# Attention plus gated FFN on one core: FFN matmuls moved from 128-row to 64-row tiles, score work cut into single units, first batch reordered

## The chip, the cores and the metric

The kernel runs on one core of one Trainium2 chip. The metric is device time in microseconds (us) of one execution, smaller is better. The names of the engines in the profile are: PE = TensorE (matmul), PEld = TensorE's weight load, DVE = VectorE, ACT = ScalarE, POOL = GpSimd, SP = SyncE, which issues most DMAs here.

## The reference

Eight batches of eight heads, sequence 576, head size 64. Causal attention with a decay per position, then a gated FFN (512 to 1536 to 512) over all 4608 tokens, in fp32 at the interface:

```python
def _attn_ref(q, k, v, f):                      # q, k, v: [8, 8, 576, 64], f: [8, 8, 576]
    scores = scale * np.matmul(q, k.transpose(0, 1, 3, 2))
    cum = np.cumsum(np.log(np.clip(f, 0.0001, 1.0)), axis=-1)
    scores = np.where(causal, -1e9, scores + cum[:, :, :, None] - cum[:, :, None, :])
    scores = scores - np.max(scores, axis=-1, keepdims=True)
    attn = np.exp(scores)
    attn = attn / (np.sum(attn, axis=-1, keepdims=True) + 1e-09)
    return np.matmul(attn, v)

def _moe_ref(x, w_gate, w_val, w_out):          # x: [4608, 512]
    return (1.0 / (1.0 + np.exp(-(x @ w_gate))) * (x @ w_val)) @ w_out
```

## The kernel before

The tokens are cut into nine FFN chunks of 512. While the FFN of chunk c runs, the attention of batch c+1 is slipped in between its matmul groups ("steps", 36 a chunk: 24 first-layer steps, 12 second-layer steps). Batches 0 and 1 are partly ahead; chunks 7 and 8 are pure FFN. Heads go in pairs, four pairs a batch.

The scores of a pair are cut into four pieces, the units A to D. They contract over the head size of 64, so the two heads stand in the two 64-row halves of the array. The FFN contracts over 128 rows.

```python
def Q_mm(p, u, sc):                       # scores: 64 rows, two heads side by side
    qT, kT = st[p, "q"], st[p, "k"]
    for jt, i0, i1, c in UNITS[u]:
        for h in range(2):
            hp = slice(64 * h, 64 * h + 64)
            nc.tensor.matmul(ps[:, sc + h, c:c + i1 - i0],
                             kT[hp, jt * NP:(jt + 1) * NP], qT[hp, i0:i1], start=True, stop=True)
...
def burst1(p):                            # two units (C and A) in one burst
    Q_mm(p, "C", 3)
    Q_mm(p, "A", 0)
    Q_exp(p, "C", 3)
    later.append(lambda: (Q_exp(p, "A", 0), vg_step(p)))
...
def burst3(p):                            # attention product of two pairs, then normalisation
    ...
    nc.vector.transpose(Z, psf[:, o:o + S])          # row sums to partitions
    nc.vector.reciprocal(r[:, 0, :], ...)
    ...                                              # copies between quadrants
    spread(1)
    later.append(one)                                # scale pair p+1
    later.append(two)                                # scale pair p
...
def g1(ft, w, kind):                      # FFN, first layer: 128 rows, one bank of three in turn
    bk = next_bank()
    for mt in range(NMT):
        nc.tensor.matmul(ps[:, bk, :], w[:, mt, ft * NP:(ft + 1) * NP],
                         xT[:, mt, t0:t0 + TCH], start=(mt == 0), stop=(mt == NMT - 1))
    if kind == "g":
        nc.scalar.activation(sg, ps[:, bk, :], ACTF.Tanh, scale=0.5)
    else:                                 # the gate product
        nc.vector.scalar_tensor_tensor(out=gv[:, ft, :], in0=hold["sg"], scalar=1.0,
                                       in1=ps[:, bk, :], op0=ALU.add, op1=ALU.mult)
...
put((0, 2, 4, 6, 9) if c == 1 else (-1, 0, 3, 6, 9), P)      # steps of the five bursts of a pair of pairs
put((15, 18, 21, 24, 27), P + 2)
```

The cuts are marked with "...".

The softmax here doesn't subtract the row's maximum and nothing guards it: scores larger than these inputs give would overflow.

Of the kernel before, what the change touches and what calls it, by code (L numbers as in the profile page):

```python
# [8 lines left out]
FP32 = mybir.dt.float32  # L9
# [6 lines left out]
def kernel(  # L16
# [14 lines left out]
    NP = 128  # L31
# [3 lines left out]
    NPAIR = BH // 2  # L35
    HPAIR = H // 2
    scale = 1.0 / float(D) ** 0.5
    TPP = 6
    QP = S // TPP

# [3 lines left out]
    NMT = DM // NP  # L44
    NFT = DF // NP
    TCH = 512
    NTC = T // TCH
    C0 = 256
# [10 lines left out]
    gsb = ctx.enter_context(tc.tile_pool(name="gv", bufs=2))  # L59
    pp = ctx.enter_context(tc.tile_pool(name="ps", bufs=1, space=bass.MemoryType.PSUM))  # L60

    ps = pp.tile([128, 8, 512], FP32, tag="ps", name="ps")

    ident_bf = singles.tile([128, 128], BF16, tag="ident_bf", name="ident_bf")
    ident_f = singles.tile([64, 64], FP32, tag="ident_f", name="ident_f")
    g_bf = singles.tile([128, NJT, BH], BF16, tag="g_bf", name="g_bf")
    xT = singles.tile([128, NMT, T], BF16, tag="xT", name="xT")
    wg_bf = singles.tile([128, NMT, DF], BF16, tag="wg_bf", name="wg_bf")
    wv_bf = singles.tile([128, NMT, DF], BF16, tag="wv_bf", name="wv_bf")
    wo_bf = singles.tile([128, NFT, DM], BF16, tag="wo_bf", name="wo_bf")  # L70
    NKT = 4
    kts = [singles.tile([128, SPAD], BF16, tag=f"kt{i}", name=f"kt{i}") for i in range(NKT)]
    NXB = 3
    qns = [singles.tile([128, 2, NJT, 2 * D], BF16, tag=f"qn{i}", name=f"qn{i}") for i in range(NXB)]
    kns = [singles.tile([128, 2, NJT, 2 * D], BF16, tag=f"kn{i}", name=f"kn{i}") for i in range(NXB)]
    NVB = 3
    vbs = [singles.tile([128, NJT, 4, D], FP32, tag=f"vb{i}", name=f"vb{i}") for i in range(NVB)]

    f_nat = singles.tile([BH, S], FP32, tag="f_nat", name="f_nat")
    cum = singles.tile([BH, S], FP32, tag="cum", name="cum")  # L80
# [5 lines left out]
    qtiles, ktiles = {}, {}  # L86

    def load_qk(b, hf, npiece):
        key = (b, hf)
        qt = qk_pool.tile([QP, 4, TPP * D], BF16, tag="qt", name="qt")  # L90
        kt = qk_pool.tile([QP, 4, TPP * D], BF16, tag="kt_in", name="kt_in")
        w = 4 // npiece
        for s in range(npiece):
            for src, dst in ((q, qt), (k, kt)):
                hs = slice(4 * hf + w * s, 4 * hf + w * s + w)
                nc.gpsimd.dma_start(
                    dst[:, w * s:w * s + w, :],
                    src[b, hs].rearrange("h (p t) d -> p h (t d)", t=TPP))
        qtiles[key], ktiles[key] = qt, kt
# [50 lines left out]
    def load_w1(gi):  # L150
        cs = slice(gi * 512, gi * 512 + 512)
        for src, dst in ((moe_w_gate, wg_bf), (moe_w_val, wv_bf)):
            nc.gpsimd.dma_start(dst[:, :, cs],
                                src.rearrange("(m p) c -> p m c", p=NP)[:, :, cs])

    def load_w2(gi):
        nc.gpsimd.dma_start(
            wo_bf[:, 4 * gi:4 * gi + 4, :],
            moe_w_out.rearrange("(m p) c -> p m c", p=NP)[:, 4 * gi:4 * gi + 4, :])


    st = {}
    later = []

    def flush():
        if later:
            later.pop(0)()
# [5 lines left out]
    def T_step(p, which, bk, copy):  # L173
        b, hf, ho = half_of(p)
        src = (qtiles if which == "q" else ktiles)[(b, hf)]
        bank = ps[:, bk, 0:S // 2].bitcast(BF16)
        for t in range(TPP):
            for h in range(2):
                nc.tensor.transpose(  # L179
                    bank[64 * h:64 * h + 64, t * QP:(t + 1) * QP],  # L180
                    src[:, ho + h, t * D:(t + 1) * D], ident_bf[0:QP, 0:QP])
        if which == "q":
            dst = tsb.tile([128, S], BF16, tag="qT", name="qT")
        else:
            dst = kts[p % NKT]
        st[p, which] = dst
        copy(dst[:, 0:S].rearrange("p (n t) -> p n t", t=TPP),
             bank.rearrange("p (t n) -> p n t", t=TPP))

# [7 lines left out]
    UW = {"A": 448, "B": 384, "C": 448, "D": 320}  # L197

    def Q_mm(p, u, sc):
        qT, kT = st[p, "q"], st[p, "k"]  # L200
        for jt, i0, i1, c in UNITS[u]:
            for h in range(2):
                hp = slice(64 * h, 64 * h + 64)
                nc.tensor.matmul(ps[:, sc + h, c:c + i1 - i0],  # L204
                                 kT[hp, jt * NP:(jt + 1) * NP], qT[hp, i0:i1],
                                 start=True, stop=True)

    def Q_exp(p, u, sc):
# [25 lines left out]


# [17 lines left out]
    def AV_mm(p, b0, b1, b2):  # L253
        av(p, CH0, b0, C0, False)
        av(p, CH0, b0, 0, True)
        av(p, CH1, b2, 0, True)
        av(p, CH1, b1, 0, False)

    def norm_r(p, b0, b1, b2):
        NB = S // 32  # L260
        Z = nsb.tile([128, S], FP32, tag="Z", name="Z")
        nc.vector.transpose(Z[:, 0:C0], ps[:, b0, 0:C0])
        nc.vector.transpose(Z[:, C0:S], ps[:, b2, 0:C1])
        r = nsb.tile([128, NB], FP32, tag="r", name="r")
        nc.vector.reciprocal(r, Z.rearrange("p (n c) -> p n c", c=32)[:, :, 0])
        R = nsb.tile([128, S], FP32, tag="R", name="R")
        nc.vector.transpose(R.rearrange("p (n c) -> p n c", c=32),
                            r.unsqueeze(2).to_broadcast([128, NB, 32]))
        st[p, "R"] = R

    def norm_m(p, b0, b1, b2):
        b, a = divmod(p, HPAIR)
        psf = ps.rearrange("p b c -> p (b c)")
        o = b0 * 512 + C0
        nc.vector.tensor_tensor(out=xT[:, a, b * S:(b + 1) * S], in0=psf[:, o:o + S],
                                in1=st[p, "R"], op=ALU.mult)


    def early_pair(p):
        Q_mm(p, "A", 0)  # L280
        Q_exp(p, "A", 0)
        Q_mm(p, "C", 2)
        Q_exp(p, "C", 2)
        if p + 1 < HPAIR:
            T_step(p + 1, "q", 4, nc.scalar.copy if p % 2 else nc.vector.tensor_copy)
            T_step(p + 1, "k", 7, nc.vector.tensor_copy)
        vg_step(p)
        if p:
            early_av(p - 1)
        Q_mm(p, "B", 0)  # L290
        Q_exp(p, "B", 0)
        Q_mm(p, "D", 2)
        Q_exp(p, "D", 2)

    def early_av(p):
        AV_mm(p, 5, 6, 7)
        norm_r(p, 5, 6, 7)
        norm_m(p, 5, 6, 7)


    def burst0(p, b0, b1):
        T_step(p, "k", b0, nc.scalar.copy)
        T_step(p, "q", b1, nc.scalar.copy)

    def burst1(p):
        Q_mm(p, "C", 3)
        Q_mm(p, "A", 0)
        Q_exp(p, "C", 3)
        later.append(lambda: (Q_exp(p, "A", 0), vg_step(p)))

    def burst2(p):
        Q_mm(p, "B", 3)
        Q_mm(p, "D", 0)
        Q_exp(p, "B", 3)
        later.append(lambda: Q_exp(p, "D", 0))
# [3 lines left out]
    def burst3(p):  # L319
        NB = S // 32  # L320
        psf = ps.rearrange("p b c -> p (b c)")
        for ch, bank, off in ((CH0, 3, C0), (CH1, 4, 0)):
            n = len(ch)
            for x, (u, c, w, jt, oc) in enumerate(ch):
                for qd in range(4):
                    pr, h = p + qd % 2, qd // 2
                    nc.tensor.matmul(  # L327
                        ps[32 * qd:32 * qd + 32, bank, off + oc:off + oc + w],
                        g_bf[:, jt, 2 * pr + h:2 * pr + h + 1].to_broadcast([128, 32]),
                        st[pr, u][:, h, c:c + w], start=(x == 0), stop=(x == n - 1),  # L330
                        skip_group_check=True, tile_position=(0, 32 * qd))
        for pr, ch, bank, off in ((p + 1, CH0, 0, C0), (p + 1, CH1, 1, 0),
                                  (p, CH0, 0, 0), (p, CH1, 2, 0)):
            n = len(ch)
            for x, (u, c, w, jt, oc) in enumerate(ch):
                for qd in range(4):
                    h = qd // 2
                    nc.tensor.matmul(  # L338
                        ps[32 * qd:32 * qd + 32, bank, off + oc:off + oc + w],
                        st[pr, "vg"][:, jt, h, 32 * (qd % 2):32 * (qd % 2) + 32],  # L340
                        st[pr, u][:, h, c:c + w], start=(x == 0), stop=(x == n - 1),
                        skip_group_check=True, tile_position=(0, 32 * qd))
        Z = nsb.tile([128, S], FP32, tag="Z", name="Z")
        o = 3 * 512 + C0
        nc.vector.transpose(Z, psf[:, o:o + S])  # L345
# [198 lines left out]
```

## Time and profile before

| reading | value | view |
|---|---|---|
| median time, 4 runs | 396.68 us (396.58 to 399.07) | times |
| TensorE busy | 94% of 396.0 us | page, part 1 |
| FFN matmul, 512 columns, start to start (its pitch) | 0.216 us | timeline, pure FFN chunks |
| pure FFN chunk | 31.1 us | timeline |
| chunk with attention | 40.9 us | timeline |
| chunk 1 begins | 82.6 us | timeline |

Of the page of the kernel before, these are TensorE's busy time beside that of the other engines (us, share of the span of 396.0 us, instructions), and one row of its second part, where each digit is one fortieth of the span: the granted clock of TensorE in tenths of full speed (9 is 90% or more).

```profile
PE 370.3 (94%) x3165; PEld 174.8 (44%) x3165; DVE 163.7 (41%) x320; ACT 191.8 (48%) x286; POOL 210.8 (53%) x341
...
PEclk9988999999999999999999999999999999999999
```

TensorE is the bound, and its clock never falls after the start.

This is TensorE's timeline of the kernel before, in a chunk with attention. The columns are the start, the time until the end, engine and line, operation, tiles, shapes, count, and in brackets the idle time before and what ended it. L392 is the FFN's first layer, L204 the scores.

```profile
183.26 1.02 PE L392 MATMUL ps<-xT,wg_bf 128*128 128x512 bf16 x4 [0.71 <-DVE gv L399]
184.22 0.56 PE L204 MATMUL ps<-xq,xk 64*128 64x448 bf16 x6
184.70 1.04 PE L392 MATMUL ps<-xT,wv_bf 128*128 128x512 bf16 x4
185.58 1.03 PE L392 MATMUL ps<-xT,wg_bf 128*128 128x512 bf16 x4
186.44 1.03 PE L392 MATMUL ps<-xT,wv_bf 128*128 128x512 bf16 x4
187.40 0.47 PE L204 MATMUL ps<-xq,xk 64*128 64x320 bf16 x6
187.81 1.04 PE L392 MATMUL ps<-xT,wg_bf 128*128 128x512 bf16 x4
```

Read the starts, since ends overlap. Four FFN matmuls without a burst behind them take 0.86 (185.58 to 186.44). From 183.26 to 184.70 is 1.44, and from 186.44 to 187.81 is 1.37. So a score burst costs 0.58 and 0.51. Its columns at the FFN's pitch are 896 and 704 (the two heads run side by side), 0.37 and 0.29 us. About 0.22 us is lost at each burst, eight times a chunk. The Trainium skill, "TensorEngine Tiling (Array Packing)", Key Properties, says that changing the tiling mode drains TensorE; the trace agrees and gives the size.

TensorE's waits in the kernel before: what was waited for, us in total, times, longest us. This line is the longest one of the steady chunks.

```profile
PE ps L392 <- DVE gv L399: 4.3, 6, 0.8
```

### The profile page before, as it was taken

How to read it: one execution, taken by the hardware profiler on the slowest of the kernel's cores; microseconds unless marked ns; L12 is line 12 of the kernel's file. 1: busy time of each engine (PE TensorE's matmuls, PEld its weight loads, DVE VectorE, ACT ScalarE, POOL GpSimd, SP SyncE). 2: the span in 40 equal slices, each digit the busy share in tenths (PEclk: the TensorE clock that was granted, in tenths of full speed). 3: DMA queues.
4: the chain of work that ended last, by engine and by line, in shares of the span. 5: the costliest groups of instructions: out<-in, count | busy, mean ns of one | idle time of the engine just before them, and what ended most of it. 6: DMA issues, size and time to landing. Idle time of an engine off the chain costs nothing.

```text
span 396.0 us, 8068 instructions
## 1 busy us (share of the span) xinstructions
PE 370.3 (94%) x3165; PEld 174.8 (44%) x3165; DVE 163.7 (41%) x320; ACT 191.8 (48%) x286; POOL 210.8 (53%) x341
## 2 busy tenths in 40 slices
PE   3867999899999999999999999999999999999995
PEld 2543444434354534443444445444544454444442
DVE  5464245245543453346252725273527252421320
ACT  5651757464545555464637363727273723323321
POOL 8774184959494949494949494848580410000000
PEclk9988999999999999999999999999999999999999
DMA  9999995899776996798679987996860011002002
GB/s 159 196 200 204 196 161 32 124 177 134 97 81 117 183 86 82 100 196 100 62 112 184 121 65 111 153 154 60 90 130 7 0 55 55 0 26 81 1 23 86
DMA packets 141319, 41.59 MB, mean 105 GB/s; under 512 B 128928, under 2 KB 136608, under 8 KB 141280
## 3 DMA queue, kind: packets, MB, share of 16 engines
q0 software_dynamic: 65616, 14.17, 40.7%
q1 hardware_dynamic: 75664, 26.90, 32.0%
q8 instruction: 25, 0.41, 0.4%
q14 instruction: 14, 0.11, 0.1%
HBM read 37.90 MB, written 9.44 MB: 120 GB/s over the span
## 4 chain that ended last, share of the span: by engine, by line
PE 79%; DVE 9%; POOL 5%; ACT 4%; issue 3%; ACTq 0%; DVEq 0%; POOLq 0%
PE ps L392 41%; PE ps L407 23%; PE ps L204 7%; PE ps L338 3%; PE ps L327 3%; DVE gv L399 2%; PE ps L249 2%; DVE R L355 1%; PE ps L179 1%; DVE r L350 1%; DVE xT L361 1%; DVE Z L345 1%; POOL vg L230 1%; ACT eA L212 1%; ACT eD L212 1%
## 5 line engine op out<-in xcount | busy, mean ns | idle before, releaser
L399 DVE SCALAR_TENSOR_TENSOR gv<-sg,ps 128x512 bf16<-128x512 bf16 x108 | 73.4, 685 | 164.7 <-PE ps L392 158.5
L392 PE MATMUL ps<-xT,wg_bf 128*128 128x512 bf16 x432 | 112.0, 382 | 6.3 <-DVE gv L399 4.3
L392 PE MATMUL ps<-xT,wv_bf 128*128 128x512 bf16 x432 | 112.0, 382 | 0.0
L397 ACT ACTIVATE sg<-ps 128x512 bf16<-128x512 f32 x108 | 64.5, 597 | 98.0 <-PE ps L392 96.0
L407 PE MATMUL ps<-wo_bf,gv 128*128 128x512 bf16 x432 | 97.4, 380 | 0.0
L392 PEld LDWEIGHTS <-wg_bf 128*128 128x128 bf16 x432 | 40.3, 98 | 56.8 <-issue 12.5
L407 PEld LDWEIGHTS <-gv 128*128 128x128 bf16 x432 | 40.6, 98 | 49.5 <-issue 3.5
L392 PEld LDWEIGHTS <-wv_bf 128*128 128x128 bf16 x432 | 40.3, 98 | 49.7 <-issue 5.4
L222 POOL TENSOR_SCALAR_AFFINE_SELECT eC<-eC 128x256 bf16<-128x256 bf16 x32 | 13.0, 407 | 92.2 <-ACT eC L212 92.2
L411 ACT ACTIVATE ob<-ps 128x512 f32<-128x512 f32 x36 | 21.5, 597 | 79.5 <-PE ps L407 74.4
L230 POOL TENSOR_TENSOR vg<-vb,g_bf 128x640 bf16<-128x640 f32 x32 | 41.0, 1281 | 1.4 <-PE ps L249 1.4
L127 POOL DMA_DIRECT2D qn<-in_q_dram x48 | 37.2, 776 | 0.0
L127 POOL DMA_DIRECT2D kn<-in_k_dram x48 | 36.6, 766 | 1.3 <-issue 0.6
L212 ACT ACTIVATE eB<-ps 128x768 bf16<-128x768 f32 x32 | 25.9, 811 | 17.6 <-PE ps L204 17.6
L212 ACT ACTIVATE eA<-ps 128x896 bf16<-128x896 f32 x32 | 29.5, 921 | 1.3 <-PE ps L204 1.3
L212 ACT ACTIVATE eC<-ps 128x896 bf16<-128x896 f32 x32 | 29.2, 912 | 0.3 <-PE ps L204 0.3
L204 PE MATMUL ps<-xq,xk 64*128 64x320 bf16 (+4 forms) x288 | 25.2, 277 | 0.8 <-ACT eA L212 0.7
L345 DVE STREAM_TRANSPOSE Z<-ps 128x576 f32<-128x576 f32 x14 | 11.0, 783 | 35.6 <-PE ps L327 35.6
L222 POOL TENSOR_SCALAR_AFFINE_SELECT eA<-eA 128x512 bf16<-128x512 bf16 x32 | 21.1, 660 | 3.3 <-ACT eA L212 2.0
L212 ACT ACTIVATE eD<-ps 128x640 bf16<-128x640 f32 x32 | 22.3, 697 | 0.0
L355 DVE STREAM_TRANSPOSE R<-r 128x576 f32<-128x576 f32 x28 | 21.6, 771 | 0.4
L204 PEld LDWEIGHTS <-xk 64*128 64x128 bf16 x288 | 10.3, 94 | 24.7 <-issue 21.2
(74 smaller groups left out, 295.4 us busy)
## 6 DMA issues: line engine op xcount, KB each, us to landing
out_dram<-ob SPq DMA_DIRECT2D x36, 256.0 KB, 2.0
vb<-in_v_dram SPq DMA_DIRECT2D x64, 128.0 KB, 3.3
kn<-in_k_dram POOLq DMA_DIRECT2D x48, 64.0 KB, 3.4
qn<-in_q_dram POOLq DMA_DIRECT2D x48, 64.0 KB, 3.2
wg_bf<-in_moe_w_gate_dram POOLq DMA_DIRECT2D x3, 512.0 KB, 10.0
wv_bf<-in_moe_w_val_dram POOLq DMA_DIRECT2D x3, 512.0 KB, 13.2
wo_bf<-in_moe_w_out_dram POOLq DMA_DIRECT2D x3, 512.0 KB, 16.6
vb<-in_v_dram SPq DMA_DIRECT2D x16, 64.0 KB, 3.9
```

The lines of the kernel that those rows point to most:

```text
L127: nc.gpsimd.dma_start(dst[:, a, 0:NJT - 1, h * D:h * D + D], src[b, hs + h, 0:(NJT - 1) * NP, :].rearrange("(t p) d -> p t d", p=NP))
L204: nc.tensor.matmul(ps[:, sc + h, c:c + i1 - i0], kT[hp, jt * NP:(jt + 1) * NP], qT[hp, i0:i1], start=True, stop=True)
L212: nc.scalar.activation(e[:, :, 0:w], ps[:, sc:sc + 2, 0:w], ACTF.Exp, scale=scale)
L222: nc.gpsimd.affine_select(out=m, in_=m, compare_op=ALU.is_ge, fill=0.0, base=0, pattern=pat, channel_multiplier=-1)
L230: nc.gpsimd.tensor_tensor(out=vg, in0=vb[:, :, ho:ho + 2, :], in1=g_bf[:, :, 2 * p:2 * p + 2].unsqueeze(3).to_broadcast([128, NJT, 2, D]), ...
L345: nc.vector.transpose(Z, psf[:, o:o + S])
L355: nc.vector.transpose(Rs[x].rearrange("p (n c) -> p n c", c=32), r[:, x, :].unsqueeze(2).to_broadcast([128, NB, 32]))
L392: nc.tensor.matmul(ps[:, bk, :], w[:, mt, ft * NP:(ft + 1) * NP], xT[:, mt, t0:t0 + TCH], start=(mt == 0), stop=(mt == NMT - 1))
L397: nc.scalar.activation(sg, ps[:, bk, :], ACTF.Tanh, scale=0.5)
L399: nc.vector.scalar_tensor_tensor(out=gv[:, ft, :], in0=hold["sg"], scalar=1.0, in1=ps[:, bk, :], op0=ALU.add, op1=ALU.mult)
L407: nc.tensor.matmul(ps[:, bk, :], gv[:, ft, tt * NP:(tt + 1) * NP], wo_bf[:, ft, :], start=(ft == 0), stop=(ft == NFT - 1))
L411: nc.scalar.mul(ob, ps[:, bk, :], 0.5)
```

## The change

The intent is to let the FFN run in the same tiling mode as the scores, so that score units can be put anywhere without a drain. The contraction of 128 rows becomes two of 64, in the two halves of the array, side by side: one half computes the gate, the other the value. Each half must then see all 512 inputs in its own 64 partitions, so the upper and lower halves of the attention output, of the gate product and of the output weights are copied across by DMA ("crossed"). The score bursts of two units become single units. And the FFN now holds four of the eight banks, two for each of two gate and value pairs in turn, which leaves the score slots to share banks 0 to 3 with the attention product's sums and outputs. For this the normalisation is cut into six pieces, put on VectorE behind the FFN steps, and a score unit is held until its banks' last reader has been issued.

The core of the diff, cut:

```diff
-            for mt in range(NMT):
-                nc.tensor.matmul(ps[:, bk, :], w[:, mt, ft * NP:(ft + 1) * NP],
-                                 xT[:, mt, t0:t0 + TCH], start=(mt == 0), stop=(mt == NMT - 1))
+        for x, sl in enumerate(slots):
+            for half, bk in ((LO, fb), (HI, fb + 1)):
+                nc.tensor.matmul(ps[:, bk, :], w1[half, sl, ft * NP:(ft + 1) * NP],
+                                 xR[half, sl, t0:t0 + TCH], ...)
 ...
+    def cross_x(p, n):                                   # behind every scaling
+            for src, dst in ((LO, HI), (HI, LO)):
+                nc.sync.dma_start(xR[dst, NSL // 2 + a:NSL // 2 + a + n, r0:r0 + w],
+                                  xR[src, a:a + n, r0:r0 + w])
 ...
+    def S_unit(p, u, slot):                              # one unit, held by the chain
+        while chain and slot in chain_holds[0]:
+            pop_chain()
 ...
+        chain.extend([(zed, both), (flip, both), (lambda: spr(1), both),
+                      (lambda: scaled(p + 1, S, loc[1]), beta),
+                      (lambda: spr(0), beta), (last, set())])
 ...
+            put(6, lambda: out_two(P))
+            units = [(P + x, u) for x in (2, 3) for u in "CABD"]
+            for n, (s, (p, u)) in enumerate(zip((10, 12, 14, 15, 17, 18, 20, 21), units)):
+                put(s, lambda p=p, u=u, n=n: S_unit(p, u, n % 2))
 ...
+    def between(c):                                      # after chunk 0, no FFN work
+        if c == 0:
+            for n, (p, u) in enumerate((P + x, u) for x in (2, 3) for u in "CABD"):
+                S_unit(p, u, n % 2)
+            ...
+            out_two(P + 2)
+            ...
+            for n, u in enumerate("CABD"):
+                S_unit(P, u, n % 2)
```

## The prediction

> **What bounds the kernel now.** TensorE. The page's first part has it busy 94% of a 396.0 us span, and the chain of waits is 79% TensorE. In the pure FFN chunks at the end (chain, from 329.6) 96 first-layer matmuls take 20.72 us and 48 second-layer ones 10.36: 0.216 us per 512 columns, 31.1 us a chunk. A chunk that also carries attention repeats every 40.9 us (one first-layer group starts at 142.34, 183.26, 224.19). Its 4 pairs stream 6400 score and 9600 attention columns; at the FFN's pitch that is an estimated 6.7 us. The other 3.1 us:
> - Switches of tiling mode. From one FFN run to the next around a score burst the timeline shows 0.52 and 0.59 us, for 0.29 and 0.37 of columns: 0.22 us lost, eight times. Around the attention product 2.27 for 2.0, twice. The Trainium skill, "TensorEngine Tiling (Array Packing)", Key Properties, says that changing the mode drains TensorE; the trace agrees.
> - One TensorE wait of 0.7 to 0.9 us for VectorE, behind the normalisation.
>
> The start (FFN begins at 33.6) and the first chunk (33.6 to about 82.6) are bound by ScalarE, GpSimd and latencies.
>
> **What the change does.** Two 64-row matmuls side by side replace one of 128 rows, so 31.1 us a chunk should stand. The eight score switches go: -1.8 us a chunk, on the critical path. Six chunks: -11. Added: DMA crossings (about 2 to 3 us landing, mostly hidden) and twice as many matmul instructions (hidden).
>
> **What I think goes wrong.** The normalisation is now spread behind FFN steps on VectorE's in-order queue, and the score slots share banks with its inputs. In program order of a steady chunk: attention product at step 6; FFN groups 3 and 4; then score unit C, whose second half waits for the first scaling. VectorE runs gate product 3, Z transpose, reciprocal and copies, gate product 4, spread, scaling. From trace durations, counted from the end of the attention product: gate product 3 ends at 3.2 (two steps, tanh 0.60, product 0.65), Z and copies at 5.45, product 4 at 6.1, spread and scaling at 7.5. TensorE arrives at 3.46: waits 4.0. Unit A, two steps later, waits for the second scaling, behind gate product 5, again about 2.9. So +6.9 a chunk, less the 0.9 wait of before. The second attention product has VectorE free. Estimated steady chunk 45 to 46.5 us against 40.9: six chunks, about +30.
>
> **First batch.** Eight score units, the attention product, its normalisation and four more units now stand between chunks 0 and 1 without FFN work: about 16 us, mostly ScalarE (0.70 to 0.92 per exp) and the VectorE chain. FFN work taken into the start gives some back. I estimate chunk 1 starts at 90 to 98, not 82.6.
>
> **Predicted: 434 us; 404 to 450 should hold it 8 times in 10. Faster by over 2%: 0.11; within 2%: 0.08; slower by over 2%: 0.81.**
>
> **What would show it.** Right: FFN pitch 0.216 us per pair; no drain around score units; in each of chunks 1 to 6 two TensorE waits of about 4 and 3 us for the scaling (xR) on VectorE, at the score line; TensorE idle near 80 to 95 us. Wrong: steady period below 40 us, or those waits under 1 us.
>
> **What would make it wrong.** Side-by-side matmuls running slower or faster than 0.216 a pair; VectorE reaching the scalings earlier than I count; long waits lowering the granted clock (slower still); crossings landing late under DMA load (slower).

## The result and the profile after

The changed kernel gives correct results and takes 480.41 us (475.91 to 482.13, 4 runs), against 396.68 before. The ratio is 1.2076, with a 95% interval of 1.1977 to 1.2174. Slower was right; the time is 46 us above the prediction and 30 above the top of its range.

The page of the changed kernel, the same lines as before (the span is 477.5 us):

```profile
PE 392.9 (82%) x5005; PEld 203.3 (43%) x5005; DVE 162.7 (34%) x316; ACT 190.6 (40%) x284; POOL 211.7 (44%) x345
...
PEclk9987998767889997999599978998899889999999
```

TensorE's busy share fell by 12 points. The clock row now has dips between full stretches, also in the chunks with attention; the kernel before had none there.

The span grew by 81.5 us. Chunk 1 starts at 109.05 instead of 82.6: 26.4 in the first batch. The six chunks with attention, 1 to 6, take 301.7 instead of 247.0: 54.7. The rest takes 66.8 instead of 66.4.

TensorE's timeline of the changed kernel in a steady chunk, from the end of the attention product on (L376 is the FFN's first layer, L211 the scores; a pair of 64-row matmuls counts as two):

```profile
271.32 3.63 PE L376 MATMUL ps<-xR,w 64*128 64x512 bf16 x32
275.32 0.35 PE L211 MATMUL ps<-xq,xk 64*128 64x448 bf16 x1 [0.37 <-DVE Z L341]
278.79 0.35 PE L211 MATMUL ps<-xq,xk 64*128 64x448 bf16 x1 [3.13 <-DVE xR L251]
278.80 3.12 PE L376 MATMUL ps<-xR,w 64*128 64x512 bf16 x16
284.53 0.56 PE L211 MATMUL ps<-xq,xk 64*128 64x256 bf16 x4 [2.61 <-DVE xR L251]
284.86 3.65 PE L376 MATMUL ps<-xR,w 64*128 64x512 bf16 x16
288.27 0.55 PE L211 MATMUL ps<-xq,xk 64*128 64x320 bf16 x4
288.61 1.67 PE L376 MATMUL ps<-xR,w 64*128 64x512 bf16 x8
290.11 0.31 PE L211 MATMUL ps<-xq,xk 64*128 64x320 bf16 x2
290.24 1.90 PE L376 MATMUL ps<-xR,w 64*128 64x512 bf16 x16
291.97 0.36 PE L211 MATMUL ps<-xq,xk 64*128 64x448 bf16 x2
292.16 1.04 PE L376 MATMUL ps<-xR,w 64*128 64x512 bf16 x8
```

Three things are to be seen.

1. The tiling does what it was made for. From 291.97 to 292.16 a unit of 448 columns costs 0.19 us, which is just its columns at 0.216 per 512. No drain is left.
2. TensorE waits twice, 3.5 and 2.6 us by the brackets: 0.37 us for the transpose of the row sums (Z) and 3.13 for the first scaling (xR) on VectorE, then 2.61 for the second scaling.
3. After each wait the same FFN work takes longer. The 16 matmuls at 290.24 take 1.90; those at 278.80 take 3.12 and those at 284.86 take 3.65. The eight at 288.61 take 1.67, those at 292.16 take 1.04. That is 1.22 + 1.75 + 0.63 = 3.6 us in this chunk, beside the waits. The trace's clock record shows what it is: the granted clock was 0.50 from 279.7 to 289.9, and 1.00 before and after.

VectorE's timeline of the same stretch shows why the scaling is late (L384 is the gate product, L341 the transpose of the row sums, with reciprocal and copies left out behind it, L241 the spread, L251 the scaling):

```profile
273.89 0.69 DVE L384 SCALAR_TENSOR_TENSOR gv<-sg,ps 128x512 bf16<-128x512 bf16 x1 [4.38 <-ACT sg L383]
274.49 0.78 DVE L341 STREAM_TRANSPOSE Z<-ps 128x576 f32<-128x576 f32 x1
...
276.57 0.69 DVE L384 SCALAR_TENSOR_TENSOR gv<-sg,ps 128x512 bf16<-128x512 bf16 x1
277.18 0.77 DVE L241 STREAM_TRANSPOSE R<-r 128x576 f32<-128x576 f32 x1
277.98 0.76 DVE L251 TENSOR_TENSOR xR<-ps,R 128x576 bf16<-128x576 f32 x1
282.31 0.69 DVE L384 SCALAR_TENSOR_TENSOR gv<-sg,ps 128x512 bf16<-128x512 bf16 x1 [3.57 <-ACT sg L383]
282.91 0.77 DVE L241 STREAM_TRANSPOSE R<-r 128x576 f32<-128x576 f32 x1
283.72 0.76 DVE L251 TENSOR_TENSOR xR<-ps,R 128x576 bf16<-128x576 f32 x1
```

The row sums were ready in the banks at 271.3. VectorE sat idle for 4.38 us because the first piece of the normalisation stands behind a gate product, whose FFN group was still running. Then the second scaling, at 283.72, stands behind the next gate product (282.31), whose group TensorE had just been kept from starting. The two engines wait for each other in turn.

TensorE's waits in the changed kernel:

```profile
PE ps L211 <- DVE xR L251: 38.3, 14, 3.2
PE ps L376 <- DMA xR<-xR: 8.5, 3, 4.9
PE ps L211 <- ACT eC L217: 7.9, 4, 6.7
```

The first line is the two waits a chunk (35.0 of its 38.3 us lie in chunks 1 to 6, in 12 waits). The second and third are the first batch. Two small waits come with the new schedule, which asks for things closer to their making: for GpSimd's mask of the last unit before the attention product, and for the transposed rows of the next batch. In chunks 1 to 6 they come four times each, 3.1 and 3.2 us in all; the kernel before has neither there.

Busy time by window, one steady chunk of the kernel before and then one of the changed kernel (window, length, busy time and instructions of each engine, then clock, DMA share and GB/s):

```profile
183.00:224.00 41.00, 40.21 (x360) 18.50 (x360) 18.35 (x37) 21.54 (x32) 28.57 (x44) 1.00 0.91 114
```

```profile
206.00:254.00 48.00, 41.13 (x553) 21.88 (x550) 16.82 (x33) 20.68 (x31) 28.48 (x44) 0.89 0.89 121
```

The mean clock fell from 1.00 to 0.89 in this chunk (0.89 to 0.93 in stretches of a chunk's length between 109 and 350 us). DMA is as loaded as before.

With these numbers the steady chunk adds up: 31.1 of FFN, 6.7 of score and attention columns, 0.5 for the two changes of mode around the attention products, a wait of 4.0 (unit C was due 16 pairs at 0.216 after 271.32, at 274.78, and its second half began at 278.79) and one of 2.8 (the bracket's 2.61 and the 0.17 by which the end of an FFN run overlaps its successor), 3.6 for the slow clock, 1.4 for the two small waits (0.76 and 0.62 here). Together 50.1; the period in the trace is 49.7 to 51.2 from chunk to chunk.

In the first batch, two of the longest waits in TensorE's timeline of the changed kernel are:

```profile
41.49 7.59 PE L376 MATMUL ps<-xR,w 64*128 64x512 bf16 x38 [4.88 <-DMA xR<-xR]
...
92.78 0.50 PE L211 MATMUL ps<-qT,kt 64*128 64x320 bf16 x4 [6.71 <-ACT eC L217]
```

The first is for a crossing, the second for the exponentials of score units. Between 28 and 60 us crossings take a median of 5.1 us to land, beside weight loads that keep the DMA engines full until 48 us (a share of 1.05 in the view of busy time by window); over the whole run the median is 2.5. (The Trainium skill, "DMA: Bandwidth & Descriptors", Anatomy of one DMA, gives a fixed cost of about 2.0 us, measured for DMAs that GpSimd issues. The unloaded crossings, issued by SyncE, fit; the loaded ones take more than twice that.) From about 85.5 to 109.05, 23.5 us, TensorE has no FFN work at all.

### The profile page after: what moved, and what is told of

Its sections match the earlier page's. It is cut to its first block, busy times and chain, and to the rows that moved or that the text cites. A ratio compares the mean times of both kernels' runs of the same rounds, so it can differ in the third digit from the quotient of the medians.

```text
span 477.5 us, 11992 instructions
## 1 busy us (share of the span) xinstructions
PE 392.9 (82%) x5005; PEld 203.3 (43%) x5005; DVE 162.7 (34%) x316; ACT 190.6 (40%) x284; POOL 211.7 (44%) x345
## 5 line engine op out<-in xcount | busy, mean ns | idle before, releaser
L376 PE MATMUL ps<-xR,w 64*128 64x512 bf16 x1728 | 226.6, 407 | 8.6 <-DMA xR<-xR 8.5
L384 DVE SCALAR_TENSOR_TENSOR gv<-sg,ps 128x512 bf16<-128x512 bf16 x108 | 74.3, 688 | 245.4 <-ACT sg L383 243.6
L376 PEld LDWEIGHTS <-w 64*128 64x128 bf16 x1728 | 96.4, 100 | 123.9 <-issue 49.7
L211 PE MATMUL ps<-xq,xk 64*128 64x320 bf16 (+4 forms) x288 | 38.2, 293 | 44.7 <-DVE xR L251 38.3
L406 PE MATMUL ps<-wox,gvx 64*128 64x512 bf16 x432 | 53.1, 384 | 2.8 <-DMA wox<-wo 2.8
L406 PE MATMUL ps<-wo,gv 64*128 64x512 bf16 x432 | 52.1, 376 | 0.0
L235 POOL TENSOR_TENSOR vg<-vb,g_bf 128x640 bf16<-128x640 f32 x32 | 40.8, 1275 | 0.0
L217 ACT ACTIVATE eA<-ps 128x896 bf16<-128x896 f32 x32 | 29.4, 919 | 26.7 <-PE ps L211 26.4
L211 PEld LDWEIGHTS <-xk 64*128 64x128 bf16 x288 | 17.9, 101 | 50.3 <-issue 34.5
L406 PEld LDWEIGHTS <-gvx 64*128 64x128 bf16 x432 | 22.3, 96 | 28.1 <-issue 5.1
L406 PEld LDWEIGHTS <-gv 64*128 64x128 bf16 x432 | 21.5, 94 | 21.3
L251 DVE TENSOR_TENSOR xR<-ps,R 128x576 bf16<-128x576 f32 (+4 forms) x40 | 24.8, 635 | 2.2
L241 DVE STREAM_TRANSPOSE R<-r 128x576 f32<-128x576 f32 x32 | 24.7, 773 | 0.4
```

Of the source, the lines that this page charges most:

```text
L211: nc.tensor.matmul(ps[:, sc + h, c:c + i1 - i0], kT[hp, jt * NP:(jt + 1) * NP], qT[hp, i0:i1], start=True, stop=True)
L217: nc.scalar.activation(e[:, :, 0:w], ps[:, sc:sc + 2, 0:w], ACTF.Exp, scale=scale)
L235: nc.gpsimd.tensor_tensor(out=vg, in0=vb[:, :, ho:ho + 2, :], in1=g_bf[:, :, 2 * p:2 * p + 2].unsqueeze(3).to_broadcast([128, NJT, 2, D]), ...
L241: nc.vector.transpose(R.rearrange("p (n c) -> p n c", c=32), r.unsqueeze(2).to_broadcast([128, NB, 32]))
L251: nc.vector.tensor_tensor(out=xR[:, a, r0:r0 + n], in0=psf[:, o + i:o + i + n], in1=R[:, i:i + n], op=ALU.mult)
L376: nc.tensor.matmul(ps[:, bk, :], w1[half, sl, ft * NP:(ft + 1) * NP], xR[half, sl, t0:t0 + TCH], start=(first and x == 0), stop=(last and ...
```

## The experiments

The theory to test (T): the loss in the steady chunks comes from the schedule, that is from the normalisation's place on VectorE's in-order queue, which makes TensorE wait twice a chunk, and from the slow clock after each wait. The loss in the first batch comes from crossings and from the stretch without FFN work. The rival (R): the 64-row tiles or their crossings cost time in every chunk. A second rival says that the slow matmuls are not due to the idle time before them.

"Period" below is the distance between the last output copies of successive chunks on ScalarE, for chunks 2 to 5, where nothing is said otherwise. For the kernel before it is 40.9; for the changed kernel 49.7 to 51.2. "First output" is the start of chunk 0's last output copy: 82.3 before, 91.3 after.

| run | median us (range) | ratio to before, 95% | period | first output |
|---|---|---|---|---|
| after | 480.41 (475.91 to 482.13) | 1.2076 (1.1977 to 1.2174) | 49.7 to 51.2 | 91.3 |
| e1_units_late | 441.04 (440.13 to 443.19) | 1.1117 (1.1052 to 1.1182) | 44.2 to 44.9 | 91.5 |
| e2_chain_first | 433.10 (429.50 to 433.79) | 1.0891 (1.0818 to 1.0964) | 42.3 to 43.3 | 89.7 |
| e3_keep_warm | 459.90 (458.37 to 461.69) | 1.1599 (1.1516 to 1.1682) | 46.7 to 48.3 | 87.9 |
| e4_stores_free | 472.60 (471.08 to 474.54) | 1.1907 (1.1837 to 1.1977) | 50.7 to 51.7 | 86.3 |
| e5_rows128 | 424.94 (423.51 to 425.05) | 1.0670 (1.0637 to 1.0704) | 43.3 to 45.4 | 75.7 |
| e8_best | 413.66 (413.42 to 413.90) | 1.0399 (1.0376 to 1.0422) | 39.5 to 39.7 | 104.5 |
| e9_best_rows128 | 413.52 (411.30 to 413.98) | 1.0384 (1.0348 to 1.0421) | 41.8 | 91.0 |
| e10_loads_behind | 399.15 (396.81 to 401.50) | 1.0041 (0.9988 to 1.0094) | 39.5 | 89.4 |
| e11_loads_behind_rows128 | 400.52 (399.03 to 401.87) | 1.0062 (1.0022 to 1.0101) | 41.8 | 78.8 |
| e12_fill_first | 402.58 (400.75 to 404.98) | 1.0106 (1.0080 to 1.0133) | 39.5 to 40.1 | 94.8 |

There were no runs with the labels e6 and e7. The medians of before in the rounds of e1 to e4, of e5 to e9, of e10 and e11, and of e12 were 396.91, 397.46, 397.31 and 397.71. All kernels gave correct results.

### e1_units_late: the score units later, all else as changed

```diff
-            for n, (s, (p, u)) in enumerate(zip((10, 12, 14, 15, 17, 18, 20, 21), units)):
+            for n, (s, (p, u)) in enumerate(zip((14, 15, 16, 17, 18, 20, 22, 23), units)):
-            put(15, lambda: vg_step(P + 2))
-            put(20, lambda: vg_step(P + 3))
+            put(17, lambda: vg_step(P + 2))
+            put(22, lambda: vg_step(P + 3))
```

> Edit: in a steady chunk the eight score units of the second half stand at steps 14 to 23 instead of 10 to 21, nothing else. Theory A (score unit C and A wait for scalings that stand behind gate products on VectorE, 4.0 and 2.8 us a chunk, and the slow clock after those waits adds about 3.9): by step 14 and 16 the scalings are done or nearly, so both waits fall below 1 us, a wait of 1 to 2 us for a free FFN bank comes in their place, and six chunks save about 8 to 9 us each: about 430 us against 480. Theory B (the 64-row matmuls or the crossings themselves make the chunk long): within 5 us of 480.

Measured: 441.04, 39 us less than the changed kernel, with the tiling, the crossings and every operation kept. Two lines of TensorE's waits in this run, the longest and the one for the scaling:

```profile
PE ps L321 <- POOL eD L227: 15.9, 11, 2.8
PE ps L211 <- DVE xR L251: 5.5, 8, 1.6
```

The wait for the scaling fell from 38.3 to 5.5 us in total. It was partly turned into another: the units now come so late that GpSimd's mask of the last one (eD) is not done when the attention product wants it, 15.9 us in place of 4.7. That is as much as the 11 us by which the run missed its expectation.

### e2_chain_first: the whole normalisation at once on VectorE

```diff
             put(6, lambda: out_two(P))
+            put(6, lambda: pop_chain(6))
```

> Edit: after the first attention product of a steady chunk VectorE is given the whole normalisation at once, ahead of the next gate products, the score units stay where they are. Theory A: first scaling ends about 3.8 us after the attention product, second about 5.3; C and A wait under 0.5 us; gate product 3 comes at about 5.9 instead of 3.2, so TensorE waits about 2 us for its FFN bank: about 435 us. Theory B: within 5 us of 480. A third view, that only the distance in steps matters and not the order on VectorE, would leave it near 480 too.

Measured: 433.1, one line, 47 us less, as expected. The period is 42.3 to 43.3. The wait for the scaling is gone from the leading lines of the waits; the first line is now

```profile
PE ps L376 <- DVE gv L384: 9.6, 6, 1.7
```

which is the old wait of the kernel before (4.3 us there), longer. The likely reason, not tested alone, is that the whole normalisation now stands ahead of a gate product and the FFN has only two pairs of banks to turn over. So the place of the normalisation is shown to be the cause of most of the steady loss, and R can't be more than a small part of it.

### e3_keep_warm: TensorE kept busy during the waits

```diff
+    def warm(n):
+        for _ in range(n):
+            nc.tensor.matmul(ps[:, 0, :], w1[LO, 0, 0:NP], w1[LO, 0, 0:512], start=True, stop=True)
 ...
+            put(10, lambda: warm(14))          # just ahead of unit C
+            put(12, lambda: warm(12))          # just ahead of unit A
```

The dummy matmuls write bank 0, whose content has been read by then and which the next unit in it overwrites. They add 26 matmuls a chunk and remove nothing that TensorE waits for.

> Edit: 14 and 12 needless 64-row matmuls of 512 columns into bank 0, just before score unit C and unit A of a steady chunk, so that TensorE works through its two long waits; results unchanged. If the slow clock after the waits is a cost of its own (about 3.9 us a chunk in the trace: 16 FFN matmuls in 3.41 us instead of 1.73), the clock stays at 1.0 in those stretches and six chunks save about 3 to 4 us each: 455 to 462 us although TensorE does more. If the clock has nothing to do with the waits, or half the array does not count as work: 480 or more.

Measured: 459.9, 20.5 us less than the changed kernel, with more work. TensorE's timeline of this run at the same place (L481 is the dummy):

```profile
214.48 3.18 PE L481 MATMUL ps<-w 64*128 64x512 bf16 x14 [0.37 <-DVE Z L341]
217.50 0.80 PE L211 MATMUL ps<-xq,xk 64*128 64x448 bf16 x2
217.96 2.07 PE L376 MATMUL ps<-xR,w 64*128 64x512 bf16 x16
219.69 2.75 PE L481 MATMUL ps<-w 64*128 64x512 bf16 x12
222.80 0.37 PE L211 MATMUL ps<-xq,xk 64*128 64x256 bf16 x4 [0.36 <-DVE xR L251]
222.99 1.91 PE L376 MATMUL ps<-xR,w 64*128 64x512 bf16 x16
```

The real matmuls after the waits take 2.07 and 1.91, where they took 3.12 and 3.65. The granted clock of this run is 1.00 from 108.7 to 456 us. So the slow matmuls are due to the idle time before them. Six chunks of 3.6 us would be 21.6. From chunk 0's last output to chunk 6's the run is 18 us shorter than the changed kernel (301.8 against 319.9); the other 3 us came earlier, where this run has no edit. So the slow clock is a term of its own, of about 18 us. The changed kernel's clock record fits: in chunks 1 to 6 TensorE was busy 39.7 us at a clock of 0.50, by which I estimate a loss of half of that, 19.8 us. The Trainium skill, "TensorE: Matmul & The Clock Gate", Part 1, describes it: half clock after an idle window of about 3.4 us, full clock after about 3.4 us of sustained work. The clock record agrees with the half clock and with the length of 3.4 us: in chunks 1 to 6 of the changed kernel every stretch at 0.50 lasts 3.4, 6.8 or 10.2 us. But no single wait there was as long as 3.4 us; the longest was 3.2.

### e4_stores_free: chunk 0's row transposes behind its stores

ScalarE's timeline of the changed kernel showed the last output copy of chunk 0 standing still for 5.0 us until an earlier store had landed, and the exponentials behind it. The stores stood in SyncE's queue behind the DMA transposes of batch 2's rows.

```diff
-                if s in (26, 28):
+                if c and s in (26, 28):
                     transpose_rows(HPAIR * (c + 2) + (s - 26) // 2)
 ...
     def between(c):
         if c == 0:
+            transpose_rows(2 * HPAIR)
+            transpose_rows(2 * HPAIR + 1)
```

> Edit: in chunk 0 alone the two row transposes of batch 2 are issued after the chunk's output stores instead of before them. Theory: the stores stand behind the transposes on the in-order issue queue, the third output buffer comes free late, ScalarE waits 5.0 us for it at 86 to 91 us and TensorE 6.7 us for the exp behind it. Then about 5 us less, 475 against 480, and both waits under 2 us. Rival: that stretch is bound by the exps themselves, and nothing changes.

Measured: 472.6, 7.8 us less by the medians, and chunk 0's last output 5.0 us earlier. The wait for ScalarE's eC fell from 7.9 to 2.9 us in total. The period did not change, as it should not.

### e5_rows128: e2 with the FFN back in 128-row matmuls

```diff
-        for x, sl in enumerate(slots):
-            for half, bk in ((LO, fb), (HI, fb + 1)):
-                nc.tensor.matmul(ps[:, bk, :], w1[half, sl, ...], xR[half, sl, t0:t0 + TCH], ...)
+        slots = [sl for sl in slots if sl < NSL // 2]
+        for x, sl in enumerate(slots):
+            for w, bk in ((wg, fb), (wv, fb + 1)):
+                nc.tensor.matmul(ps[:, bk, :], w[:, sl, ...], xR[:, sl, t0:t0 + TCH], ...)
 ...   (second layer likewise; no crossing of xR, gv or wo is left)
```

> Edit: on top of e2 (433 us) the FFN goes back to 128-row matmuls, in the same order and the same places; the crossings by DMA and the crossed copies go with it; score units stay one at a time. If 64-row tiling is worth what the trace of before says (a score unit alone costs about 0.2 us more in 128-row surroundings), 16 units a chunk add about 3 us each chunk, less what the waits absorb; the first batch loses its crossing waits (6.9 us in e2): about 433 to 445. If the tiling itself were a burden on the steady chunk, its period falls below e2's and the time falls below 425.

Measured: 424.94, 8 us less than e2 and less than T expected. The period did not fall below e2's, as R would have it: it is 43.3 to 45.4 (one chunk, with 3.4 us at half clock, makes the 45.4), where e2 has 42.3 to 43.3, and from chunk 0's last output to chunk 6's this run is 9.6 us longer (281.2 against 271.6). So the 64-row tiling saves time in the steady chunks of this schedule too, about 1 us a chunk in chunks 2 to 5, less than the 3 us that the expectation started from; VectorE's gate product is the longest wait in both (8.5 us in total here, 9.6 in e2). The gain is in the first batch: without crossings chunk 0's last output comes at 75.7 instead of 89.7. R is right there and only there.

### e8_best and e9_best_rows128: a mended schedule, with and without the tiling

This schedule changes only places. The first three pieces of the normalisation go to VectorE at once and the rest behind the next two gate products; the units start at step 12; batch 1's attention is spread through chunk 0 so that no stretch is left without FFN work; row loads and transposes come earlier. e9 is the same with 128-row FFN matmuls and no crossings.

```diff
+        pop_chain(now)                          # now = 3 in the first layer
 ...
-            put(6, lambda: out_two(P))
+            put(6, lambda: out_two(P, 3))
-            ... zip((10, 12, 14, 15, 17, 18, 20, 21), units)
+            ... zip((12, 14, 15, 16, 17, 18, 20, 21), units)
 ...
-            for n, (p, u) in enumerate((P + x, u) for x in (2, 3) for u in "CABD"):
-                S_unit(p, u, n % 2)             # no longer between the chunks
 ...
+            load_v(1, 0, nc.gpsimd)             # in the loop over batch 0's pairs
```

> Edit: the change with its schedule mended. Normalisation: first three operations right behind the attention product, the rest behind the next two gate products; score units from step 12; batch 1 spread through chunk 0 instead of standing between chunks 0 and 1; transposes two to four steps earlier; row loads spread. Expected from the theory: steady chunk 39.5 to 40.5 us (31.1 + 6.7 + two switches of the attention product 0.5 + about 1 of waits), no cold clock from chunk 1 on; chunk 1 starts at 86 to 92; 395 to 405 in all. If chunk 1's start stays above 100, the first batch is bound by something other than the stretch without FFN work.

> Edit: e8 with the FFN in 128-row matmuls, no crossings. This tells the tiling apart on a schedule without long waits: 16 single score units a chunk, each with two switches of mode, cost about 0.2 us each: steady chunk about 3 us longer than in e8, six chunks 15 to 20 us; the first batch 5 to 10 us shorter for want of crossings. In all 5 to 15 us above e8. If the switch costs nothing, it is 5 to 10 us below e8.

Measured: 413.66 and 413.52. The period of e8 is 39.5 to 39.7, as expected and below the 40.9 of the kernel before. That of e9 is 41.8. With the VectorE waits gone, the tiling is worth 2.2 us a chunk. The two timelines show it at one unit of 448 columns. First e8, then e9:

```profile
188.20 0.35 PE L211 MATMUL ps<-xq,xk 64*128 64x448 bf16 x2
188.39 1.03 PE L379 MATMUL ps<-xR,w 64*128 64x512 bf16 x8
```

```profile
192.66 0.38 PE L376 MATMUL ps<-xR,wv 128*128 128x512 bf16 x1
192.97 0.36 PE L210 MATMUL ps<-xq,xk 64*128 64x448 bf16 x2
193.26 0.39 PE L376 MATMUL ps<-xR,wg 128*128 128x512 bf16 x1
```

In e8 the unit costs 0.19. In e9 0.60 passes from one FFN matmul to the next; less 0.216 for the first of them and 0.19 for the unit, the change of mode and back costs 0.19.

The totals missed the expectation because of my own edit. TensorE's first wait in e8 is

```profile
PE ps L379 <- DMA xR<-xR: 20.4, 3, 17.2
```

SyncE's timeline shows why: the loads of batch 1's values, which wait for GpSimd, ran from 31.7 to 40.8, and the crossings of the last two pairs, which were behind them in the same queue, were issued only at 40.9.

### e10_loads_behind and e11_loads_behind_rows128: that edit taken back

```diff
-            load_v(1, 0, nc.gpsimd)
 ...
     out_one(HPAIR - 1, 1, 2, 3)
+    load_v(1, 0)                                # behind the crossings, no gate
 ...
-                if s == 4:
-                    load_v(1, 1, nc.gpsimd)
-                if s == 21:
+                if s == 8:
+                    load_v(1, 1)
+                if s == 14:
                     cross_w2()
```

> The version with the mended schedule, with my own mistake taken out: the second batch's first value loads no longer stand ahead of the last pairs' crossings in SyncE's queue (they follow them), and the crossing of the down-projection's weights is issued seven steps earlier. Theory (the 17.2-us wait of TensorE for the crossing in the first batch was caused only by the queue order, and the steady chunks owe nothing to it): the wait falls to about 5 us, the 3.7-us wait for the crossed down-projection weights goes, the steady period stays at 39.5; total 413.7 less 12 less 3 to 4 = 397 to 402. Rival (the crossing waits because the DMA engines are full in the first batch, whatever the order): the wait stays above 12 us and the total above 408.

> The same schedule and loads with the FFN in 128-row matmuls and no crossings at all. Theory: steady period stays at 41.8 (2.3 over the 64-row version, times about 6 chunks = 14 us), the 9.6-us wait for GpSimd's mask in the first batch goes because the value loads are no longer gated by GpSimd behind its weight loads: 413.5 less 9 = 402 to 407, so 2 to 8 us slower than the 64-row twin. If the crossings cost the first batch more than the tiling saves later, it is instead level with the twin or faster.

Measured: 399.15 and 400.52, 14.5 and 13 us less; e10 lies in the expected range, e11 just below it. In e10 the wait for the crossings is

```profile
PE ps L379 <- DMA xR<-xR: 8.3, 2, 5.2
```

So the queue order had caused most of it, not the DMA traffic alone. e11 has no crossings and gained from the same edit in another way: in e9 TensorE stood 9.6 us for GpSimd's mask in the first batch, and in e11 that wait is gone. Between the two versions the first output differs by 10.5 us (89.35 against 78.82) in favour of 128 rows, and the period by 2.3 in favour of 64. That nearly cancels over this kernel's length. Both are level with the kernel before, within 2%.

### e12_fill_first: work put into the waits for crossings

The last pair's attention product is issued before the matmuls that wait for the second pair's crossing; batch 1's transposes and its first four units stand in front of the matmuls that wait for the last crossing; the attention products of chunk 0 come one step later.

```diff
-    g1_slots(0, 0, (0, 4, 1, 5), True, False)
+    g1_slots(0, 0, (0, 4), True, False)
     out_one(HPAIR - 1, 1, 2, 3)
     load_v(1, 0)
-    g1_slots(0, 0, (2, 6), False, False)
+    g1_slots(0, 0, (1, 5, 2, 6), False, False)
     g1_slots(0, 1, (0, 4, 1, 5, 2, 6), True, False)
+    T_step(HPAIR, 0, 1, ACTC, DVEC)
+    T_step(HPAIR + 1, 2, 3, ACTC, DVEC)
+    for n, u in enumerate("CABD"):
+        S_unit(HPAIR, u, n % 2)
```

> The mended version with three more edits in the first batch only: the last pair's attention product is issued before the FFN matmuls that wait for the second pair's crossing (so its own crossing starts some 3 us earlier); the second batch's transposes and its first pair's four score units stand before the FFN matmuls that wait for the last crossing, so TensorE works while it flies; the two attention products of chunk 0 come one step later, so that GpSimd's masks are done. Theory (what is left of the loss against before is TensorE idle in the first 90 us, 8.3 us for crossings and about 5 us for masks): 399.2 less 6 to 9 = 390 to 393, with the steady period still 39.5, and the ratio to before under 1. Rival (the first batch is paced by DMA traffic and the idle time moves to another wait): 397 or more, with new waits of about the same sum before 90 us.

Measured: 402.58, no gain (1.0106 to before, where e10 has 1.0041). The rival of this run was right: the waits moved. The wait for xR fell to 4.9 us, and a new one came up at the crossing of the gate product:

```profile
PE ps L409 <- DMA gvx<-gv: 6.3, 4, 5.1
```

The first 32 FFN matmuls after the filled stretch also take 6.2 us (42.84 to 49.04), where 3.5 are due at 0.216 a pair. The stretch in front of them was broken by five waits of 0.3 to 2.6 us, and the granted clock was 0.50 from 34.4 to 48.1.

No version is faster than the kernel before.

## Why the prediction was right or wrong

- **What bounds the kernel before, and the gain of the tiling: right.** The drain that was to go did go (0.19 for a unit of 448 columns, its columns alone), and the pure FFN chunks at the end still take 31.1 us. By e9 against e8 the tiling is worth 2.2 us a chunk, but with 16 single units that would each switch modes; the prediction's 1.8 was for the eight bursts of the kernel before. Against that kernel the period of e10 is 1.4 us shorter (39.5 against 40.9).
- **Two waits a chunk of 4.0 and 2.9 us: right.** They are 4.0 and 2.8 in the chunk shown, with the mechanism as predicted, and e2 takes them away with one line.
- **"Estimated steady chunk 45 to 46.5 us": wrong, the step that failed.** It is about 50. The sum left out a term that the prediction named only as a risk ("long waits lowering the granted clock"): 3.6 us a chunk in the trace, and about 18 us in all by e3. It also left out two small waits, 1.4 us together in the chunk shown and 6.3 over chunks 1 to 6, for GpSimd's mask and the transposed rows. Six chunks cost 54.7 us where the prediction had about 30. The two terms, about 18 us and 6.3 us over the six chunks, make 24 of the 25 that were missing. These are about 25 of the 46 us by which the number was off; most of the rest is the first batch.
- **"I estimate chunk 1 starts at 90 to 98": wrong in size.** It starts at 109.05. Idle time near 80 to 95 us was there as predicted, but the sum treated the crossings as mostly hidden at 2 to 3 us. In the first 60 us they took about 5, and TensorE waited 8.5 us for them. The output stores behind the row transposes in SyncE's queue, worth 5.0 to 7.8 us by e4, were not seen at all. By e5 against e2 the 64-row version with its crossings delays chunk 0's output by 14.0 us in e2's schedule. How the 26.4 us divide exactly between crossings, slow clock and the stretch without FFN work was not settled, since these overlap.
- **The probabilities** put 0.81 on slower, and slower it was.

The full drop from 480 to 399 us was reached without changing a single operation of the FFN: by places in queues alone.

## What to carry to other kernels

When waits of a few microseconds appear in front of TensorE, put the slow clock after them into the sum: here 7 us of waits in a chunk brought 3.6 us of slow matmuls. When a change moves work to an in-order engine, write out that engine's order and look for pairs of engines that wait for each other in turn; the cheapest mend is to issue at once what others wait for. A gain in the steady part (2.3 us a chunk here) must be set against what its preparation costs at the start (10.5 us), and with six repeats the two can cancel.

## What the Trainium skill lacked or had wrong

- "TensorEngine Tiling (Array Packing)", Key Properties, says that a change of mode drains TensorE, and gives no size. The runs show about 0.2 us for a switch to 64 rows and back (0.22 a burst before, 0.19 for a single unit in e9), and no loss between FFN and score tiles of the same 64-row mode (0.19 us for 448 columns).
- "TensorE: Matmul & The Clock Gate", table under "Why this matters for your kernels", advises no TensorE gaps over about 3 us. Shorter waits, with no other wait of 1 us within 10 us before them, were followed by half clock here: one of 2.40 us in e10 (until 80.91, then a granted clock of 0.50 from 81.8 to 85.2) and one of 1.47 us in e5 (until 241.36, then 0.50 from 242.3 to 245.7). That wait of 1.4 to 1.5 us comes once in each of e5's chunks 1 to 5, and the other four left the clock at 1.00. So a gap under 3 us can cost the clock but need not; where a limit lies is not shown.
- The same page advises to warm up before a benchmark; no page says that dummy matmuls during a wait pay inside a kernel. In e3 26 of them a chunk saved about 18 us over chunks 1 to 6.
- "DMA: Bandwidth & Descriptors", Anatomy of one DMA, gives a fixed cost of about 2.0 us for DMAs issued by GpSimd. For copies from on-chip memory to on-chip memory issued by SyncE, no page has a time from issue to landing: the crossings took a median of 2.5 us over the run and 5.1 between 28 and 60 us, beside weight loads.
